# Rebuilding the weight-gradient part of a fused attention and MLP backward kernel in the transposed layout

## The chip, the cores and the metric

The kernel runs on one core of one Trainium2 chip. The metric is the device time of one execution in microseconds (us). A kernel's time is the median of its runs. Each experiment was timed in 3 or 5 rounds beside the kernel before, on the same chip. A ratio is the mean time of one kernel's runs over that of the other's runs of the same rounds, so it isn't quite the ratio of the medians quoted beside it. A profile is one execution; stage lengths come from profiles. Most vary by one or two us from run to run (the pause before dx took 55.9 to 57.2 us in five profiles whose runs don't touch it); the output loop of the changed kernel varies by more, 98.9 to 109.0 us in five profiles with the same loop, nearly all of it in one stall (below).

Engine names as the profile has them: PE is TensorE (matrix products), PEld its weight loads, DVE is VectorE, ACT is ScalarE, POOL is GpSimd, SP is SyncE, which here only issues DMAs. PEclk is the granted TensorE clock as a share of full speed. "DMA share" is the mean busy share of the core's 16 DMA engines (overlapping packets let it go over 1).

## The reference

One attention block and one MLP, joined by a gate, and the gradients of everything. S = 2048 rows, D = 512 columns, 32 heads of 16, F = 1792 hidden columns, all bfloat16.

```python
def _A_ref(x, wqkv, wo):                 # 32 heads of 16, softmax attention
    ...
    return (...).reshape(B, S, D) @ wo
def _B_ref(x, w1, b1, w2, b2):
    y = _layernorm(x)
    h = _gelu(jnp.einsum("bsd,df->bsf", y, w1) + b1)      # tanh form of gelu
    return jnp.einsum("bsf,fd->bsd", h, w2) + b2
xn = _layernorm(x)
s = _A_ref(xn, A_wqkv, A_wo)
g = _silu(_B_ref(xn, B_w1, B_b1, B_w2, B_b2))
out = x + s * g
# wanted: out and jax.vjp for x, wqkv, wo, w1, b1, w2, b2
```

## The kernel before

The program has three parts. A first part (0 to 280 us) makes layer norms, projections and the MLP forward. A hand-scheduled attention, forward and backward in one (280 to 2190 us), follows. The tail (2190 to 2780 us) makes the output, the MLP backward and all weight gradients. The change rewrites the tail.

In the tail, the MLP backward walks over 16 tiles of 128 rows. The hidden activations h lie transposed in DRAM (F on the rows), so each tile is turned on TensorE first, the gelu slope is computed in row layout, and the gradient is turned back for the next product:

```python
def stage_a(t):                              # gelu and its slope for 128 rows
    nc.sync_or_scalar.dma_start(out=h1T[:], in_=k.H1T_s[:, t*128:(t+1)*128]...)   # cut
    for ci, (f0, fn) in enumerate(FCH):      # 14 PE transposes, copied by DVE or ACT
        nc.tensor.transpose(pt[:, b, :], h1T[:, ci*4 + b, :], k.ident_bf[:])
    ... # 2 ACT passes, 3 POOL passes, 5 DVE passes over [128, 1792]
    nc.sync.dma_start(out=k.HG_s[t*128:(t+1)*128, :], in_=hg[:])     # gelu(h), rows
def stage_b(t):
    for ci, (f0, fn) in enumerate(FCH):
        ...                                  # 4 products dm @ w2T into ps
        nc.vector.tensor_tensor(out=dh1[:, f0:f0+fn], in0=ps[:, 0:fn], in1=gp[:, f0:f0+fn], op=ALU.mult)
        for b in range(nb):                  # 14 PE transposes back
            nc.tensor.transpose(pt2[:, b, :], dh1[:, f0+b*128:...], k.ident_bf[:])
        nc.scalar.copy(out=dh1T[:, ci*4:ci*4+nb, :], in_=pt2[:, 0:nb, :])
    nc.scalar.dma_start(out=k.DH1_s[t*128:(t+1)*128, :], in_=dh1[:])
    nc.vector.reduce_sum(out=db1acc[:, t, :], in_=dh1T[:], axis=AX.X)
    ...                                      # 14 products dh1T @ w1T into ps
    ln_bwd_tile(nc, wk, ps[:], y_all[:, t, :], k.rstd2[:, t:t+1], None, dxm_all[:, t, :])
stage_a(0)
for t in range(NT):
    if t + 1 < NT:
        stage_a(t + 1)
    stage_b(t)
```

The layer-norm gradient of a tile runs mostly on POOL, in up to five steps:

```python
def ln_bwd_tile(nc, wk, dy_ps, xhat_bf, rstd_col, extra_add, out_ap, ...):
    ...                                      # row sums s1 (ACT or DVE) and s2 (DVE)
    nc.gpsimd.tensor_scalar(out=ns2[:], in0=s2[:], scalar1=-1.0/D, ...)
    nc.gpsimd.tensor_scalar(out=nms1[:], in0=s1[:], scalar1=-1.0/D, ...)
    nc.gpsimd.tensor_scalar(out=prod[:], in0=xhat_bf, scalar1=ns2[:, 0:1], ...)
    nc.gpsimd.tensor_tensor(out=prod[:], in0=prod[:], in1=dyf[:], op=ALU.add)
    nc.gpsimd.tensor_scalar(out=out_ap, in0=prod[:], scalar1=nms1[:, 0:1], scalar2=rstd_col, ...)
```

The output loop before it keeps the gate tensors of all tiles in memory, turns all 16 tiles of the attention output first, and only then multiplies:

```python
for t in range(NT):
    transpose_to(nc, psT, oT, k.Oall[:, t, :], k.ident_bf, IC, t, t)
for t in range(NT):
    ...                                      # ps = oT(t) @ wo
    nc.vector.tensor_tensor(out=t1[:], in0=ps[:], in1=g_all[:, t, :], op=ALU.mult)
    ...                                      # out = x + t1, stored
    nc.vector.tensor_tensor(out=dm_all[:, t, :], in0=ps[:], in1=B_all[:, t, :], op=ALU.mult)
    transpose_to(nc, psT, dmT, dm_all[:, t, :], k.ident_bf, IC, t, 1)
```

The order of the tail is: output, dwo, weight transposes, MLP backward, dw2, dw1, then dx and dwqkv (with 64 PE transposes of dQ and 128 of dKV).

## Time and profile before

The kernel took 2779.34 us (median of 3 runs, 2777.35 to 2779.35). The profiled execution spans 2779.8 us.

The table of windows gives the busy time of each engine (with instruction counts) in each stretch, then the granted clock, the DMA share and the DMA rate. Kernel before; the first row shown is the attention, then come the stages of the tail: output with dwo and weight transposes, MLP backward, a pause, dw2, dw1, a pause, and the last part.

```profile
core 0: us, PE busy (x) PEld busy (x) DVE busy (x) ACT busy (x) POOL busy (x), PEclk, DMA share, GB/s
...
280.00:2190.00 1910.00, 1773.95 (x15632) 480.41 (x15633) 1548.66 (x2625) 1471.57 (x1538) 267.58 (x699) 0.99 1.15 228
2190.00:2258.00 68.00, 54.09 (x373) 29.78 (x371) 29.37 (x55) 22.55 (x39) 18.65 (x17) 0.90 0.64 212
2258.00:2497.00 239.00, 155.54 (x930) 79.84 (x928) 192.64 (x228) 110.67 (x163) 184.10 (x126) 0.85 0.30 93
2497.00:2521.00 24.00, 1.44 (x12) 1.20 (x12) 1.10 (x2) 1.90 (x1) 2.41 (x3) 0.55 0.50 123
2521.00:2588.00 67.00, 54.22 (x223) 22.26 (x224) 4.84 (x7) 3.52 (x6) 0.00 (x0) 0.91 0.71 176
2588.00:2640.00 52.00, 49.19 (x263) 25.45 (x260) 5.76 (x11) 4.85 (x9) 0.00 (x0) 0.99 0.32 99
2640.00:2663.00 23.00, 4.15 (x41) 3.56 (x40) 1.18 (x3) 4.01 (x8) 0.00 (x0) 0.57 1.01 360
2663.00:2780.00 117.00, 98.78 (x572) 49.41 (x570) 64.03 (x115) 15.66 (x32) 54.88 (x80) 0.98 0.10 33
```

Attention keeps PE busy for 93% of 1910 us, so there is little to win. The tail is 590 us, and its largest piece is the MLP backward: 239 us, in which DVE (192.6 us) and POOL (184.1 us) are busier than PE (155.5 us).

The table of waits says what TensorE stood still for. Kernel before, the tail from 2258 us on:

```profile
engine line waited for: us in total, times, longest us
PE dh_tp L421 <- DVE dh L418: 74.6, 31, 15.7
PE ps_dw L448 <- DMA hgc<-HG_s: 29.2, 9, 16.6
PE kv_tp L509 <- DMA Rkv<-dKVT_s: 18.6, 1, 18.6
```

The first line is the cost of the row layout. TensorE can't turn the gradient back before DVE has multiplied by the slope, and DVE is late. The longest waits of the two lines after it (16.6 and 18.6 us) lie in the two pauses.

### The profile page before, as it was taken

The page shows a single profiled execution, that of the slowest core. Times are in us where ns is not written, and L with a number is a line of the kernel's source. Part 1 is how long each engine was busy: PE and PEld are TensorE (multiplying, and loading weights), DVE is VectorE, ACT ScalarE, POOL GpSimd, SP SyncE. Part 2 cuts the span into 40 slices and gives each one's busy share as a digit, 9 for nine tenths or more (in the row PEclk, how much of TensorE's full clock was granted, in tenths as well). Part 3 has the DMA queues.
Part 4 walks back from the last instruction along what each step waited for, and adds up shares of the span by engine and source line. Part 5 has one row for each costly group of instructions (what it writes and reads, how often), then busy time and mean ns, then how long its engine had stood idle before and what let it go on. Part 6 is the DMA issues. An engine that isn't in the chain of part 4 may idle for free. (4 is left out here: it accounts for less than half of the span.)

```text
span 2779.8 us, 48839 instructions
## 1 busy us (share of the span) xinstructions
PE 2373.2 (85%) x18944; PEld 777.2 (28%) x18944; DVE 2012.5 (72%) x3382; ACT 1736.5 (62%) x1973; POOL 620.4 (22%) x1023
## 2 busy tenths in 40 slices
PE   3786999999999999999999999999999856766967
PEld 2332122222222222222222222222222333322443
DVE  5764688888888888888888888888888638870144
ACT  3343677777777777777777777777777534440020
POOL 0434011111111110111101111111111328870034
PEclk8898799999999999999999999999999978887989
DMA  5434999999999999999999999999999753226331
GB/s 181 108 127 131 197 221 235 226 234 228 231 228 231 236 222 235 225 230 231 230 238 229 226 235 226 234 228 230 227 233 217 208 169 103 96 96 161 106 132 42
DMA packets 1823500, 543.41 MB, mean 195 GB/s; under 512 B 1746593, under 2 KB 1807394, under 8 KB 1823266
## 3 DMA queue, kind: packets, MB, share of 16 engines
q1 hardware_dynamic: 1749874, 486.66, 85.2%
q10 hardware_dynamic: 73392, 53.62, 6.3%
q8 instruction: 148, 2.42, 0.4%
q14 instruction: 86, 0.70, 0.1%
HBM read 65.41 MB, written 55.32 MB: 43 GB/s over the span
## 5 line engine op out<-in xcount | busy, mean ns | idle before, releaser
L699 DVE TENSOR_TENSOR gts<-d,et 128x512 bf16<-128x512 f32 x2048 | 1301.8, 681 | 329.4 <-issue 293.9
L678 ACT ACTIVATE et<-s 128x1024 bf16<-128x1024 f32 x1024 | 997.2, 1023 | 13.1 <-PE d L664 11.7
L686 ACT ACTIVATE e<-t 128x1024 bf16<-128x1024 f32 x512 | 524.3, 1024 | 422.2 <-PE t L636 421.2
L664 PE MATMUL d<-QDT,KVT 32*128 32x512 bf16 x2048 | 597.6, 381 | 115.8 <-DVE gts L699 114.8
L650 PE MATMUL s<-QDT,KVT 32*128 32x512 bf16 x2048 | 401.5, 389 | 14.6 <-DMA QDT<-QDPad 12.6
L730 PE MATMUL X<-et,Lc 128*32 128x512 bf16 x2048 | 401.4, 389 | 14.0 <-DVE xs L751 14.0
L733 PE MATMUL X<-et,NAT 128*32 128x512 bf16 x2048 | 402.0, 389 | 0.0
L745 PE MATMUL X<-gts,NAT 128*17 128x512 bf16 x2048 | 400.5, 387 | 0.0
L814 PE MATMUL Z<-gk,W 128*32 128x512 bf16 x2048 | 394.6, 379 | 0.0
L778 POOL TENSOR_TENSOR W<-NATQd,rL 128x128 bf16<-128x128 bf16 x64 | 25.8, 403 | 1340.7 <-DVE rL L773 1340.7
L745 PEld LDWEIGHTS <-NAT 128*17 128x17 bf16 x2048 | 92.5, 87 | 492.5 <-issue 492.5
L808 PE MATMUL Z<-e,W 128*32 128x512 bf16 x1024 | 200.4, 385 | 3.4 <-DVE acc L821 2.3
L808 PE MATMUL Z<-ek,W 128*32 128x512 bf16 x1024 | 201.3, 389 | 0.0
L636 PE MATMUL t<-KVT,QDT 32*128 32x512 bf16 x1024 | 199.1, 385 | 0.0
L650 PEld LDWEIGHTS <-KVT 32*128 32x128 bf16 x2048 | 96.6, 91 | 356.6 <-issue 356.5
L664 PEld LDWEIGHTS <-KVT 32*128 32x128 bf16 x2048 | 140.1, 91 | 68.5 <-issue 36.9
L730 PEld LDWEIGHTS <-Lc 128*32 128x32 bf16 x2048 | 103.8, 93 | 179.8 <-issue 179.8
L821 DVE TENSOR_TENSOR acc<-Z,acc 64x512 f32<-64x512 f32 x192 | 129.2, 673 | 10.7 <-PE Z L814 10.7
L808 PEld LDWEIGHTS <-W 128*32 128x32 bf16 x2048 | 120.9, 93 | 56.4 <-issue 50.6
L733 PEld LDWEIGHTS <-NAT 128*32 128x32 bf16 x2048 | 100.6, 95 | 50.6
L814 PEld LDWEIGHTS <-W 128*32 128x32 bf16 x2048 | 103.6, 95 | 8.0
L826 POOL CAST ob<-acc 64x512 bf16<-64x512 f32 x64 | 38.8, 607 | 295.3 <-DVE acc L821 295.3
(200 smaller groups left out, 2600.9 us busy)
## 6 DMA issues: line engine op xcount, KB each, us to landing
gk<-gts SPq DMA_TRANSPOSE x512, 4.1
HG_s<-hg SPq DMA_DIRECT2D x16, 448.0 KB, 2.9
DH_s<-dh ACTq DMA_DIRECT2D x16, 448.0 KB, 2.5
NAT<-NAT_s SPq DMA_DIRECT2D x16, 264.0 KB, 3.3
GB_s<-gB ACTq DMA_DIRECT2D x16, 256.0 KB, 2.0
ek<-et SPq DMA_TRANSPOSE x256, 4.2
dKVT_s<-ob SPq DMA_DIRECT2D x16, 256.0 KB, 3.5
dhc<-DH_s ACTq DMA_DIRECT2D x2, 2048.0 KB, 13.2
```

Source lines behind the costliest of these rows:

```text
L636: nc.tensor.matmul(t[:, hj, :], lhsT=op["QDT"][r:r + 32, q0:q0 + 128], rhs=op["KVT"][r:r + 32, kc * 512:(kc + 1) * 512], start=True, stop= ...
L650: nc.tensor.matmul(s[:, hj, :], lhsT=op["KVT"][r:r + 32, kb * 128:(kb + 1) * 128], rhs=op["QDT"][r:r + 32, qc * 512:(qc + 1) * 512], start ...
L664: nc.tensor.matmul(d[:], lhsT=op["KVT"][r:r + 32, kb * 128:(kb + 1) * 128], rhs=op["QDT"][r:r + 32, qc * 512:(qc + 1) * 512], start=True, ...
L678: nc.scalar.activation(out=et[:, :, kb % 4, :, :].rearrange("k b h q -> k h b q"), in_=st_s.pop(g)[:].rearrange("k h (b q) -> k h b q", b= ...
L686: nc.scalar.activation(out=e[:], in_=st_t.pop(g)[:], func=ACT.Exp)
L699: nc.vector.tensor_tensor(out=gts[:, kb % 2, hj, :].rearrange("k (b q) -> k b q", b=4), in0=ds[hj][:].rearrange("k (b q) -> k b q", b=4), ...
L730: nc.tensor.matmul(X[64 + 32 * hj:96 + 32 * hj, :], lhsT=Lc[:], rhs=et[:, :, kb % 4, hj, :], start=(kb == 0), stop=False, skip_group_check ...
L733: nc.tensor.matmul(X[32 * hj:32 * hj + 32, :], lhsT=NATt[:, kb, hj, 1:33], rhs=et[:, :, kb % 4, hj, :], start=(kb == 0), stop=(kb == 15), ...
L745: nc.tensor.matmul(X[64 + 32 * hj:64 + 32 * hj + 17, :], lhsT=NATt[:, kb, hj, 0:17], rhs=gts[:, kb % 2, hj, :], start=False, stop=(kb == 1 ...
L808: nc.tensor.matmul(Z[32 * hj:32 * hj + 32, :], lhsT=blk[j]["W1"][:, qb, hj, :], rhs=ev[:, hj], start=(qb == qb_order[0]), stop=False, tile ...
L814: nc.tensor.matmul(Z[32 * hj:32 * hj + 32, :], lhsT=blk[j]["W2"][:, qb, hj, :], rhs=gv[:, :, :, hj, qb, :], start=False, stop=(qb == qb_or ...
L821: nc.vector.tensor_tensor(out=av, in0=Z[0:64, :], in1=av, op=ALU.add)
```

## The change

The intent: keep the MLP backward in the transposed layout (F on the partitions) from end to end. Then h needs no transpose, the slope is computed on the tensor as it lies, and the two products of the MLP backward chain without turning anything. What must be turned (gelu(h) for dw2, dh for dw1, the weights, dQ, dKV) goes through DMA transposes from DRAM, all on the SP queue. The bias gradient becomes an accumulation in the product's own instruction; the layer norm leaves POOL; the MLP's gradient is added to dx by a product with the identity. To make room in on-chip memory, gate tensors and inputs are loaded per tile, and the output loop becomes one loop per tile, with two of four slope sets free to run beside it. (A slope set holds the gelu slopes of 512 rows, in 7 groups; there are 28 groups in all.) The core of the diff, cut:

```diff
+    def emit_gp(sc):                        # gelu slope, 512 rows, transposed
+        for f0, nf in FG:                   # 7 groups of [128, 2, 512]
+            nc.scalar.dma_start(out=h1[:], in_=k.H1T_s[f0*128:(f0+nf)*128, sc*512:(sc+1)*512]...)
+            ...                             # 3 ACT passes, 7 DVE passes, no POOL
-    for t in range(NT):
-        transpose_to(nc, psT, oT, k.Oall[:, t, :], k.ident_bf, IC, t, t)
     for t in range(NT):
+        transpose_to(nc, psT, oT, k.Oall[:, t, :], k.ident_bf, IC, 0, t)
         ...                                 # ps = oT @ wo
+        (nc.sync if t % 2 == 0 else nc.scalar).dma_start(out=gb[:], in_=k.GB_s[t*128:(t+1)*128, :, :])
         ...                                 # dm, out, dmT as before
+        if t == 3:
+            nc.sync.dma_start_transpose(out=w2T[:], in_=B_w2)
+            nc.sync.dma_start_transpose(out=w1T[:], in_=B_w1)
+    emit_gp(0)
     ...                                     # dwo
+    emit_gp(1)
+    ...                                     # dw2, gelu(h) by nc.sync.dma_start_transpose(out=hgc[:], in_=k.HGT_s[...])
-    stage_a(0)                              # and the row-layout loop over 16 tiles
+    for sc in range(4):                     # 512 rows at a time
+        for fc in range(FC):
+            ...                             # ps = w2T(fc) x dmT
+            nc.vector.scalar_tensor_tensor(out=dh[:, fc, :], in0=ps[:], scalar=1.0, in1=gp[:, fc, :],
+                                           op0=ALU.mult, op1=ALU.mult, accum_out=db1acc[:, sc, fc:fc+1])
+        nc.sync.dma_start(out=k.DH1T_s[:, sc*512:(sc+1)*512]..., in_=dh[:])
+        for tl in range(4):
+            ...                             # ps = dh x w1T, layer-norm gradient
     nc.sync.dma_start(out=out_5.rearrange("(c p) -> p c", p=128), in_=db1[:])
-    ...                                     # PE transposes of wqkv, dQ and dKV
+    nc.sync.dma_start_transpose(out=wT[:], in_=A_wqkv)
+    nc.sync.dma_start_transpose(out=dQT[:], in_=k.dQ_s)
+    nc.scalar.dma_start(out=R[:], in_=k.dKVT_s...)          # then xn_all, dQn
+    nc.sync.dma_start_transpose(out=dKVn[:], in_=k.dKVT_s)
     ...                                     # dx and dwqkv, then dw1 with dhc by DMA transpose
```

The layer norm's new tail end: two tiny DVE operations, one ACT pass with scale and bias, one DVE product (and a POOL addition only in the last part).

## The prediction

> **What bounds the kernel now.** The table of windows splits the 2780 us into three parts: before attention (0 to 280), attention (280 to 2190) and the tail that computes the weight gradients (2190 to 2780, 590 us). The change leaves attention alone except that its gradient store is cut into four small DMAs per pair. In attention the PE is 93% busy, and I expect it unchanged within 10 us. All the gain must come from the tail.
>
> In the tail the PE is busy about 415 of 590 us, and its clock sinks to 0.76 to 0.9 in stages with gaps. The timeline and chain of waits show where the 590 us go: output, dwo and weight transposes 68; the tile loop of the MLP backward 239 (15 us a tile, a ring of POOL, DVE, ACT and PE: POOL ops of 1.5 to 2.6 us, DVE products slowed to 1.2 to 1.7 us beside POOL, a 2.0 us reduction per tile, 448 PE transposes with their copies); 24 of PE idle for a tiny store (15.7 us) and the first reload; dw2 67 with 2 to 5 us DMA waits between columns; dw1 49; 23 of idle for the reload of dKVT; the last part 117, where 76 us are the layer-norm ring on POOL (4.4 us a tile).
>
> **What the change removes.** About 800 of 928 PE transposes (0.06 us each when dense) and their copies; the reduction (now an accumulation in the product); POOL from the gelu slope and nearly all of the layer norm; the dependence between tiles.
>
> **What it adds.** 25 MB of DMA transposes from DRAM on the SP queue. Attention moves 512 KB transposes at 230 GB/s, landing in 4.1 us; the Trainium skill, "DMA: Bandwidth & Descriptors", section "Latency and other measured facts", gives 261 GB/s. From the trace's rate I estimate 4.6 us per MB, so 115 us in all, mostly hidden. That DRAM sources run like SBUF sources is not shown by this trace. Also added: two 3.7 MB stores of the gelu output before attention (0 to 5 us), a dQ round trip, a second sigmoid.
>
> **New tail by stage (estimates).** A dense 512-column matmul costs 0.216 us (dw1 stage).
> 1. Output loop: PE needs 25 us, but the order of instructions puts two of four gelu-slope sets between its DVE products: 14 groups of about 4.4 us (scaled from the 1.09 us uncontended 1792-wide product) plus 26 us: DVE-bound, 85 us, against 68 before.
> 2. dwo and dw2: 288 matmuls, 62 us, plus 3.
> 3. MLP backward: 448 matmuls, 97 us; DVE catches up on the last slope groups: 107.
> 4. Gap: transposed weight, dQ and 4 MB of dKVT must land after the MLP part: 27 of PE idle.
> 5. dx and dwqkv: 400 matmuls, 86 us, with 12 waiting for the 4 MB transposed dKV: 100. dw1: 49. End: 3.
> Sum 434 to 440 instead of 590: about 150 us saved, all on the critical path, since the tail is serial.
>
> **Predicted: 2625 us, range 2560 to 2700.** Faster by over 2%: 0.93; within 2%: 0.05; slower: 0.02.
>
> **What would show it.** Right: MLP backward near 107 us with PE clock above 0.95; no idle over 2 us between dw2 columns; DVE over 85% busy in the output loop while PE is under half; PE idle 20 to 35 us before dx; POOL under 60 us in the tail; attention still 1910 us.
>
> **What would make it wrong.** DRAM transposes at half the assumed rate: then dw2, the gap and dw1 wait on DMA, and up to 90 us are lost (2700). Loads behind 9 us transposes in the SP queue starving the output loop. Better: DVE groups shorter, or the clock at 1.0 throughout (2570). Wrong results from transposes are not expected: all run on one queue.

## The result, and the profile after

The changed kernel took 2690.18 us (median of 4 runs, 2684.70 to 2701.22) against 2778.72 us for the kernel before in the same rounds: ratio 0.969, 95% interval 0.966 to 0.972. Executions over 1.5% slower than the fastest of the same kernel are left out of the means. It is faster by 3.1%, within the predicted range, but 65 us over the predicted point. The profiled run was the fastest of the four (2684.70).

The table of windows of the kernel after (columns as before); the rows shown: attention, output loop, dwo with dw2, MLP backward, a pause, dx with dwqkv, dw1.

```profile
280.00:2190.00 1910.00, 1768.16 (x15620) 480.01 (x15620) 1547.99 (x2624) 1470.54 (x1537) 267.56 (x698) 0.99 1.15 228
2190.00:2292.00 102.00, 55.49 (x201) 18.85 (x202) 76.89 (x126) 53.01 (x62) 22.24 (x16) 0.51 0.76 192
2292.00:2365.00 73.00, 67.31 (x298) 29.22 (x296) 44.00 (x77) 43.13 (x52) 1.53 (x1) 0.95 0.74 162
2365.00:2471.00 106.00, 100.35 (x447) 44.36 (x446) 79.71 (x221) 33.94 (x57) 0.00 (x0) 0.95 0.32 95
2471.00:2527.00 56.00, 1.11 (x6) 0.30 (x4) 3.40 (x10) 2.20 (x4) 0.00 (x0) 0.55 1.06 263
2527.00:2624.00 97.00, 90.14 (x399) 39.96 (x398) 36.75 (x92) 23.69 (x48) 20.51 (x16) 0.95 0.44 119
2624.00:2683.00 59.00, 50.95 (x447) 44.00 (x445) 6.53 (x15) 5.22 (x14) 0.00 (x0) 0.97 0.56 123
```

The balance of the tail, stage against stage, in us:

| | before | predicted | after | after minus predicted |
|---|---|---|---|---|
| output loop | in the next row | 85 | 102 | +17 |
| dwo, dw2 (before: with output and weight transposes) | 68 + 67 | 65 | 73 | +8 |
| MLP backward | 239 | 107 | 106 | -1 |
| PE idle between stages | 24 + 23 | 27 | 56 | +29 |
| dx, dwqkv | 117 | 100 | 97 | -3 |
| dw1 and end | 52 | 52 | 59 | +7 |
| tail | 590 | 436 | 493 | +57 |

The MLP backward does what was hoped: 133 us less, PE busy 95% of it at clock 0.95. Not all of the 133 us is saved work, though: the last operation of a slope group (L319, counted by windows) ran 12 times in the output loop, 9 times in dwo with dw2 and only 7 times in the MLP backward, so 21 of the 28 groups, at some 4.5 us of DVE each, were done before the stage began. Two stages give a part back: the output loop at clock 0.51, and one long pause.

In the views of the loop, dm is the gradient that enters the MLP backward, oT the turned attention output of a tile, and gb a tile's two gate tensors. The waits of TensorE in the output loop, kernel after (columns as in the waits before):

```profile
PE tp_ps L52 <- DVE dm_all L346: 24.6, 15, 12.0
PE ps_so L340 <- DVE oT L54: 16.8, 8, 12.9
PE ps_so L340 <- ACT oT L56: 5.5, 8, 0.7
```

Every turn waits twice, for the product (dm_all) and for a copy (oT). Two waits stand out. The first product waits 12.9 us for a copy that stands on DVE behind slope operations, whose input was still being loaded, and one turn waits 12.0 us for dm while the gate loads stand behind the weight transposes (run 3). The timeline of one turn of that loop, kernel after (start, length, engine, operation; weight loads, slope operations and DMA issues left out), shows why:

```profile
2261.97 0.68 DVE L346 TENSOR_TENSOR dm_all<-ps_so,gb 128x512 bf16<-128x512 f32 x1
...
2262.71 0.61 PE L52 MATMUL tp_ps<-ident_bf,dm_all 128*128 128x128 bf16 x4 [1.13 <-DVE dm_all L346]
2263.25 0.58 PE L353 MATMUL psdb<-dm_all,ones_bf 128*1 128x512 bf16 x1
...
2263.76 0.61 PE L52 MATMUL tp_ps<-ident_bf,Oall 128*128 128x128 bf16 x4
2264.41 0.42 DVE L54 COPY oT<-tp_ps 128x512 bf16<-128x512 bf16 x1 [0.83 <-PE tp_ps L52]
2264.89 1.89 PE L340 MATMUL ps_so<-wo_sb,oT 128*128 128x512 bf16 x4 [0.52 <-DVE oT L54]
2266.82 0.69 DVE L346 TENSOR_TENSOR dm_all<-ps_so,gb 128x512 bf16<-128x512 f32 x1 [0.78 <-PE ps_so L340]
```

This is a ring. PE multiplies, DVE makes dm, PE turns dm, PE turns the next tile of the attention output, DVE or ACT copies it, PE multiplies. From product to product it takes 4.85 us (2261.97 to 2266.82), and the four products take 1.89 us because TensorE is at half clock (1.03 us in turns of run 5 where the clock is up). The first wait, the stall and 16 such turns (some 77 us) are the 102 us of the loop. In the five profiles with this loop the stall took 9.6 to 17.5 us and the rest 89.3 to 91.5 us.

The waits of TensorE from the pause on, kernel after:

```profile
PE ps_dxa L457 <- DMA dQT<-dQ_s: 54.9, 1, 54.9
PE ps_dwq L446 <- DMA dKVn<-dKVT_s: 6.9, 1, 6.9
PE ps_dw L474 <- DMA dhc<-DH1T_s: 4.4, 2, 2.7
```

### The profile page after: what moved, and what is told of

Its sections match the earlier page's. It is cut to its first block, busy times and chain, and to the rows that moved or that the text cites. A ratio compares the mean times of both kernels' runs of the same rounds, so it can differ in the third digit from the quotient of the medians.

```text
span 2682.9 us, 47705 instructions
## 1 busy us (share of the span) xinstructions
PE 2317.8 (86%) x18320; PEld 743.1 (28%) x18320; DVE 1960.5 (73%) x3502; ACT 1733.7 (65%) x1951; POOL 404.5 (15%) x831
## 4 chain that ended last, share of the span: by engine, by line
PE 37%; DVE 37%; issue 14%; DMA 7%; POOL 2%; ACT 1%; SPq 1%; ACTq 0%; DVEq 0%; POOLq 0%
DVE gts L640 29%; PE d L605 6%; PE X L686 6%; PE Z L755 4%; PE Z L749 3%; PE t L577 2%; DVE xs L692 2%; DVE xt L704 2%; PE ps_dhg L405 2%; PE ps_dwq L446 2%; PE XT L702 1%; PE X L671 1%; PE ps_h L212 1%; PE ps_dw L474 1%; PE ps_dw L384 1%
## 5 line engine op out<-in xcount | busy, mean ns | idle before, releaser
L671 PE MATMUL X<-et,Lc 128*32 128x512 bf16 x2048 | 398.0, 385 | 14.3 <-DVE xs L692 14.3
L762 DVE TENSOR_TENSOR acc<-Z,acc 64x512 f32<-64x512 f32 x192 | 129.2, 673 | 13.3 <-PE Z L755 13.3
L577 PEld LDWEIGHTS <-QDT 32*128 32x128 bf16 x1024 | 48.2, 91 | 202.3 <-issue 202.3
```

What stands on the lines that cost most here:

```text
L577: nc.tensor.matmul(t[:, hj, :], lhsT=op["QDT"][r:r + 32, q0:q0 + 128], rhs=op["KVT"][r:r + 32, kc * 512:(kc + 1) * 512], start=True, stop= ...
L671: nc.tensor.matmul(X[64 + 32 * hj:96 + 32 * hj, :], lhsT=Lc[:], rhs=et[:, :, kb % 4, hj, :], start=(kb == 0), stop=False, skip_group_check ...
L762: nc.vector.tensor_tensor(out=av, in0=Z[0:64, :], in1=av, op=ALU.add)
```

## The experiments

Twelve kernels ran, all with results that match the reference. Stage lengths are read from their profiles the same way as above.

### 1. The bias gradient stored in rows (db1rows)

db1 has 1792 values of two bytes. The kernel stores them element by element, while the last tile's y (for the layer norm that must end before anything of the last part may overlay its memory) is being fetched. The edit turns the sums on TensorE and stores 14 rows of 256 bytes.

```diff
-db1 = wk.tile([128, FC], bf16, name="db1")
-nc.vector.tensor_copy(out=db1[:], in_=db1f[:])
-nc.sync.dma_start(out=out_5.rearrange("(c p) -> p c", p=128), in_=db1[:])
+nc.tensor.transpose(db1p[0:FC, 0:128], db1f[:], k.ident_f[:])
+nc.vector.tensor_copy(out=db1[:], in_=db1p[0:FC, 0:128])       # [14, 128]
+nc.sync.dma_start(out=out_5.rearrange("(c p) -> c p", p=128), in_=db1[:])
```

> The changed kernel with one edit: the gradient of b1 is turned by one small PE transpose and stored as 14 rows of 256 bytes, where it was stored as 1792 single elements of 2 bytes (15 us in the DMA rings, 19 to 31 GB/s moved meanwhile). Theory (the element-wise store holds up the rings, so that the last load of a y tile takes 17.5 us, so the last layer-norm tile ends late, so the next part's buffers come free late): the last y load lands in under 4 us, the first dx matmul starts 12 to 17 us earlier, the PE gap before it falls from 55 to 38 to 43 us, the whole by 12 to 17 us (about 2675 us). Rival (the DMA transposes themselves choke the y load): the y load still takes over 12 us and the time stays within 4 us.

Measured: 2678.98 us, ratio 0.9635 (0.9617 to 0.9654), against 0.9687 for the kernel after. The pause went from 56.2 to 45.3 us. Loads of y, kernel after, from the view of that tile (time from issue to landing over the 16 loads):

```profile
DMA to landing us min/median/max: 2.0/2.1/17.5
```

The same of db1rows:

```profile
...
DMA to landing us min/median/max: 2.0/2.0/5.2
```

And the DMA view of the kernel after in 2467 to 2481 us, when that last load was on its way:

```profile
DMA packets 1108, 0.35 MB, mean 25 GB/s; under 512 B 1012, under 2 KB 1108, under 8 KB 1108
```

Little moves in these 14 us, at a DMA share of 0.76. By queue, 996 of the packets (0.25 MB) are on SP's, where the first dh transpose is under way, and 112 (0.10 MB) on ACT's, the y load: this is the traffic that was held up, not the store itself. How the store is cut is seen in the kernel before, where it has SP's queue to itself: the DMA view of 2497 to 2513 us counts 1808 packets with 0.00 MB on that queue, for 1792 values. The Trainium skill, "DMA: Bandwidth & Descriptors", section "Rules for kernel authors", says that a non-contiguous last dimension lowers to one descriptor per element; this trace agrees. In the kernel after, the store of 3.5 KB took 21.3 us to land and held up a 128 KB load that takes 2.1 us otherwise. This is 11 us of the pause, shown; how so small a store holds the others up is not.

### 2. The first dh transposes later (dhclate)

Next to that store, two transposes of dh (for dw1) were issued some 150 us before their use. Were they what delayed the y load?

```diff
-nc.sync.dma_start_transpose(out=dKVn[:], in_=k.dKVT_s)
+last_tr = nc.sync.dma_start_transpose(out=dKVn[:], in_=k.dKVT_s)
 ...
+with tc.issue_after(last_tr.ins):
     nc.sync.dma_start_transpose(out=dhc[:], in_=k.DH1T_s[f0:f0 + 256, :])
```

> The changed kernel with one edit: the first two transposed loads of dh for the dw1 part are queued behind the transposes of the qkv weight, dQ and dKV, not ahead of them. Theory (the element-wise store is the culprit of the first 15 us, and the rest of the gap is bandwidth for the operands of the next part, which can't be loaded before the last layer-norm tile is done): the last y load still takes over 12 us, the gap falls by 0 to 5 us only. Rival (the order in the SP queue costs the gap): the y load lands in under 4 us, the gap falls by 15 to 20 us.

Measured: 2685.68 us, ratio 0.9661 (0.9644 to 0.9678). The last y load still took 14.3 us, the pause was 52.0 us. So the transposes count for some 4 us, and the element-wise store for the larger part.

### 3. The weight transposes later (wlate)

In the output loop, the loads of the gate tensors stand behind the transposes of w2 and w1 on the SP queue (11.7 and 8.1 us of issue in the kernel after).

```diff
-if t == 3:
-    nc.sync.dma_start_transpose(out=w2T[:], in_=B_w2)
-    nc.sync.dma_start_transpose(out=w1T[:], in_=B_w1)
+if t == 12:
+    with tc.issue_after(o0_dma.ins):         # behind tile 12's output store
+        ...                                  # the same two
```

> The changed kernel with one edit: the transposed loads of w2 and w1 (20 us of the SP queue) are queued behind the output store of tile 12, not after tile 3. Theory (the output loop of 101 us holds 12 us of waiting for loads stuck behind these two; beyond that it is bound by VectorE): no PE wait over 5 us at tile 5, the loop takes 88 to 94 us, the whole falls by 6 to 12 us. Rival (the loop is bound by VectorE alone, and the wait only moves its work): loop within 4 us of 101.

Measured: 2675.67 us, ratio 0.9625 (0.9606 to 0.9644). The loop went from 101.8 to 92.8 us (98.9 to 109.0 in the five profiles with the old order). The 12 us stall at tile 5 is gone: no wait for dm is longer than 2.0 us. The rest of the loop still runs at half clock (0.52) with its ring.

### 4. A slope set moved out of the loop (gplate)

The prediction called the loop DVE-bound, since slope operations run beside it. This edit keeps the second set behind the loop's last product.

```diff
-emit_gp(1)
+with tc.issue_after(last_dve.ins):          # last_dve: t1 of the last tile
+    emit_gp(1)
```

> The changed kernel with one edit: the second gelu-slope set may not start before the output loop's last product on VectorE. Theory (in the loop VectorE is in order and works on slopes that are not needed for another 100 us, while PE waits): the loop falls from 101 to 75 to 82 us; the MLP backward grows from 110 to 115 to 130, as VectorE has 233 us of work from the end of attention to the gap against PE's 184; net 8 to 20 us faster. Rival (the total of VectorE's work bounds this stretch, wherever it is placed): the loop shrinks, the MLP part grows by the same, the whole within 4 us.

Measured: 2702.04 us, ratio 0.9717 (0.9698 to 0.9735), no faster than the kernel after (0.9687; the intervals overlap, so it isn't shown to be slower). This is the run that takes the prediction's model of the loop down. Its loop, table of windows (columns as before):

```profile
2190.00:2298.00 108.00, 53.35 (x197) 18.50 (x200) 54.25 (x89) 37.74 (x47) 19.93 (x16) 0.53 0.76 169
```

DVE work fell from 76.9 to 54.3 us, and the loop did not shrink. Its 108.1 us hold a stall of 17.8 us; without the stall it is 90.3 us, against 89.8 us in the kernel after. The slopes came back in the MLP backward, which rose from 106.3 to 118.4 us.

### 5. The loop staggered over three tiles (pipe)

Same instructions, only TensorE's order is fixed: turn the attention output of tile t, multiply tile t-1, turn dm of tile t-2. (oT gets three buffers of its own.)

```diff
-for t in range(NT):
-    ...                                     # turn O(t), multiply, turn dm(t)
+for i in range(NT + 2):
+    if i < NT: stage_o(i)                   # transposes of O(i), copy to oT
+    if 1 <= i <= NT: stage_s(i - 1)         # products, dm, t1, output
+    if i >= 2: stage_m(i - 2)               # transposes of dm, db2 product
+    # each TensorE instruction: tc.keep_in_program_order(...)
```

> The changed kernel with the output loop staggered over three tiles: in each turn TensorE transposes the attention output of tile t, multiplies tile t-1, and transposes the product of tile t-2; the same instructions, only TensorE's order is fixed. Theory 'one in-order ring': the output loop (101.8 us, VectorE busy 76.5 us of it) is long because every tile runs TensorE, VectorE, TensorE, copy, TensorE in sequence, so the loop falls to about 78 to 85 us (then VectorE's own work holds it) and the whole to about 2668 to 2675 us. Rival 'VectorE's order': the slope operations that stand ahead of the products on VectorE, and their loads, set the pace; the loop stays above 95 us and the whole above 2683 us.

Measured: 2672.14 us, ratio 0.960 (0.9585 to 0.9614). Table of windows, the loop of this run:

```profile
2190.00:2273.00 83.00, 39.82 (x205) 17.89 (x206) 48.46 (x81) 32.98 (x42) 19.77 (x16) 0.63 0.89 213
```

The loop fell from 101.8 to 82.2 us, as the ring theory has it. A part of this is the rival's: the first product starts 6.8 us after the attention's last, against 13.3 us in the kernel after, since the first copies no longer stand behind slope operations on DVE. And a part came back: only 5 slope groups ended in this loop, 10 were left for the MLP backward (7 in the kernel after), and that stage took 114.6 us. But my reason for stopping at 80 us, DVE's own work, is wrong: DVE is busy for 48.5 of 83 us. The largest wait of TensorE in this loop:

```profile
PE tp_ps L373 <- DVE dm_all L362: 32.9, 5, 13.2
```

There are five waits for dm now, up to 13.2 us long, not one per tile. What DVE itself waits for in the same loop is the gate tensors' loads (same view, DVE):

```profile
DVE dm_all L362 <- DMA gb<-GB_s: 19.1, 4, 10.0
```

In the timeline, these loads stand behind the w2 and w1 transposes on SP.

### 6. Staggered, and the slope set out of the loop (pipegp)

The edits of 5 and 4 together.

> The staggered loop, and the second set of gelu slopes kept behind the loop's last product on VectorE. Theory 'one in-order ring': without those slopes the staggered loop has about 45 us of VectorE work and falls to 55 to 65 us; but the slopes come back in the MLP stage (118 us in the earlier run with only this move, against 106), so the whole is 2660 to 2672 us, within 10 us of the staggered loop alone. Rival 'TensorE at the low clock holds the loop': some 4 us of TensorE per tile at half clock keep the loop at 65 us or more whatever VectorE has to do, and the whole is above 2675 us.

Measured: 2669.91 us, ratio 0.9592 (0.9575 to 0.961). The loop took 77.1 us, the MLP backward 115.0 us. Neither theory has both numbers: the loop isn't at 55 to 65 us, and the whole isn't above 2675 us. The edit moved little, since in run 5 too only 5 slope groups ended in the loop; so this run says little about DVE. The granted clock rose to 0.73 (0.63 in run 5) and the loop fell by 5 us only, so half clock is not the whole limit of this version. I took the loads to be: DVE waits 18.1 us for gate tensors, and the DMA share is 0.94 at 227 GB/s. Run 10 tests that.

### 7. Two operands of the last part fetched early (early)

db1rows, plus the transposed attention weights (1.5 MB) and dQ (2 MB) fetched during the MLP backward into memory of their own.

```diff
+pR = c1.enter_context(tc.tile_pool(name="p3_early", bufs=1, side="right"))
+wT = pR.tile([128, 12, D], bf16, name="wqkvT"); dQT = pR.tile([128, IC, S], bf16, name="dQT")
 for sc in range(4):
     ...
+    if sc == 1:                             # behind the dh store
+        nc.sync.dma_start_transpose(out=wT[:], in_=A_wqkv)
+        nc.sync.dma_start_transpose(out=dQT[:], in_=k.dQ_s)
```

> The changed kernel with the 14-row bias store and with the transposed attention weights and the transposed query gradient (1.5 and 2 MB) fetched during the MLP stage into memory of their own, so that they aren't part of the burst at the stage change. Theory 'bytes of the burst': the gap before the first input-gradient product falls from 45 us (bias store alone) to 18 to 26 us, and the whole from 2679 to 2652 to 2662 us. Rival 'a serial chain after the last layer norm': the gap stays at 38 us or more and the whole within 8 us of 2679 us.

Measured: 2661.40 us, ratio 0.9553 (0.9533 to 0.9572), against 0.9635 for db1rows. The first dx product follows the MLP backward at once, and the waiting moved inside the last part, which grew from 95.6 to 116.4 us. The pause is thus about 21 us (0.5 + 116.4 - 95.6) instead of 45.3: the theory of bytes holds in this sum, though the gap itself, 0.5 us, is not where the theory had it. The MLP backward grew by 7 us to 113.5; why, I didn't settle.

What these bytes are is seen in the DMA view of the kernel after, 2489 to 2527 us, the second part of its pause:

```profile
DMA packets 21558, 12.65 MB, mean 333 GB/s; under 512 B 16310, under 2 KB 20534, under 8 KB 21558
...
Rkv<-dKVT_s ACTq DMA_DIRECT2D x1, 4096.0 KB, 13.5
xn_all<-XN_s ACTq DMA_DIRECT2D x1, 2048.0 KB, 20.3
dQn<-dQ_s ACTq DMA_DIRECT2D x1, 2048.0 KB, 26.9
```

For 38 us the DMA engines are full (share 1.10) and TensorE has nothing to do. The 1.5 MB transpose of the weights, first in the SP queue, took 25 us to issue because it shared the engines with 8 MB of plain loads, and dQT waited behind it.

### 8. Only the new layer norm, in the old kernel (newln)

The layer-norm gradient leaves POOL and the MLP's gradient is added by an identity product; everything else is the kernel before. The function is the new one shown under the change; the call sites:

```diff
-ln_bwd_tile(..., k.rstd1[:, t:t+1], dout_all[:, t, :], dx[:], add_src=dxm_all[:, t, :])
+nc.tensor.matmul(ps[:], lhsT=k.ident_bf[:], rhs=dxm_all[:, t, :], start=True, stop=False)
+ln_bwd_tile(..., k.rstd1[:, t:t+1], dx[:], extra_add=dout_all[:, t, :])
```

> The kernel before with only one part of the change: the layer-norm gradient moved off GpSimd (the new five-step form), and the MLP gradient added through an identity product. If the layer norm on GpSimd (81 of its 184 us in the MLP stage, 55 us in the last) is what held those stages, the MLP stage falls from 239 to about 200 us, the last from 117 to about 103 us, and the whole to 2715 to 2730 us. If it is VectorE (192 of 239 us busy, and the new form gives it one operation more per tile) and the transposes of the row layout, the MLP stage stays above 220 us, and the whole is 2745 us or more: then the layout, not the layer norm, is where the saving came from.

Measured: 2773.98 us against 2784.46, ratio 0.9967 (0.9952 to 0.9981). Its MLP backward, and its last part, from the table of windows:

```profile
2251.00:2504.00 253.00, 161.77 (x981) 89.47 (x998) 196.33 (x276) 125.29 (x184) 104.14 (x48) 0.81 0.32 94
...
2674.00:2776.00 102.00, 97.36 (x560) 49.47 (x568) 52.52 (x114) 36.93 (x79) 20.29 (x16) 0.99 0.11 37
```

POOL lost 79 us in the MLP backward, and that stage became longer: 253 us against 243 for the same stretch (2251 to 2494) before. The last part did become 14 us shorter. So the layer norm was not what cost the 239 us. That the row layout was, with DVE at 196 us and TensorE waiting for it, follows by elimination only: its transposes, its reduction and its slope work were not taken out one at a time.

### 9. The old layer norm in the changed kernel (oldln)

```diff
-nc.vector.tensor_scalar(out=ab[:, 0:1], ...)     # and the rest of the new form
+nc.gpsimd.tensor_scalar(out=ns2[:], ...)         # the old form, on POOL
```

> The changed kernel with only the layer-norm gradient put back on GpSimd in its old form. Theory 'the new layout, not the layer norm, made the MLP stage short': GpSimd has about 5 us a tile, 81 us in the MLP stage of 106 us, where it is otherwise idle, so the stage grows by no more than 8 us; the last part grows by 5 to 15 us, because its tiles come every 3.4 us in fours; the whole is 2695 to 2710 us. Rival 'the layer norm is a large part of the gain': MLP stage and last part together grow by 30 us or more, the whole above 2718 us.

Measured: 2702.58 us, ratio 0.9704 (0.9684 to 0.9724), against 0.9687 for the kernel after: 5 us by the ratios, whose intervals overlap, and 12 by the medians. The MLP backward took 110.2 us (106.3), as expected; the last part did not grow (95.8 us), though I had expected 5 to 15 us; dw1 took 62 us instead of 56, which I can't explain. In the new layout the place of the layer norm is nearly free.

### 10. A version meant to beat both (best)

The staggered loop, the weight transposes behind tile 12, the rows of db1, and dw1 moved: right after the MLP backward, with y and two blocks of dh fetched before, so that the operands of the last part load while TensorE has work. dwqkv starts at tile 9.

```diff
+y_all = pR.tile(...); dhp2 = ...(bufs=2, side="right")     # in the MLP stage
+if sc == 3: load_dhc(0); load_dhc(1)
+for ci in range(7):                          # dw1 before dx
+    ...                                      # 4 x 16 products, 4 stores
+    if ci + 2 < 7: load_dhc(ci + 2)
+    ...                                      # wT after block 0, dQT after block 1, dKVn in 4 pieces from block 4
-if t % 4 == 3: dw_qkv(t // 4)
+if t >= 9 and t % 2 == 1: dw_qkv((t - 9) // 2)
```

> The version meant to beat both: the changed kernel with the staggered output loop, the transposes of the MLP weights moved behind the loads of tile 12, the 14-row bias store, and the weight gradient dw1 done right after the MLP stage (its operand y and the first two blocks of dh fetched during that stage into memory of their own), so that the 14 MB for the last part load while TensorE has work; the products for dwqkv come from tile 9 on. If the output loop is held by its in-order ring and by loads behind the weight transposes, it falls to 60 to 72 us (from 101.8). If the gap is bytes waiting with no work left, it goes to the end of dw1 and shrinks to 10 to 20 us (from 56), as some 66 us of transfers stand against 50 us of products. The whole: 2600 to 2630 us. If instead one serial queue of transposes (some 46 us of issue for dw1's and the two operands of dx) holds dw1, that stage is over 75 us instead of 56, and the whole is 2630 us or more.

Measured: 2652.89 us, ratio 0.9522 (0.9498 to 0.9547). The output loop:

```profile
2190.00:2254.00 64.00, 34.36 (x210) 15.74 (x207) 39.98 (x64) 25.54 (x35) 18.81 (x16) 0.80 0.86 208
```

It took 63 us, at clock 0.80, so staggering the ring and moving the weight transposes together took off 39 of its 102 us. Some slope work left the loop with them (DVE is busy 40 us in it, against 77), but run 4 showed that this alone gains nothing. But dw1 took 97 us instead of 56, as the second alternative had it, and the whole missed 2600 to 2630. The waits of the tail:

```profile
PE ps_dw L490 <- DMA dhc<-DH1T_s: 34.6, 5, 15.9
PE tp_ps L373 <- DVE dm_all L362: 22.6, 6, 14.8
PE ps_dhg L446 <- DVE dh1T L448: 17.0, 7, 6.3
```

The third line is a shorter loop's price: DVE's slope work (some 4.5 us a group, 28 groups) is the same, and what isn't done beside the loop is done in the MLP backward, now 123 us.

### 11. The same with staggered loads (best2)

The 8 MB of plain loads no longer start together, but one by one behind dw1's copies; the third slope set may start before dw2, and y is loaded from SP's queue instead of ACT's.

```diff
-nc.scalar.dma_start(out=R[:], ...); nc.scalar.dma_start(out=xn_all[:], ...); nc.scalar.dma_start(out=dQn[:], ...)
+if ci in act_loads:                          # R in halves at 0 and 1, xn at 2, dQn at 5
+    with tc.issue_after(act_copy.ins):
+        act_loads[ci]()
```

> The version before with two edits: the 8 MB of loads for the last part are no longer issued at once at the end of the MLP stage but one by one behind copies of the dw1 blocks (4 MB in two halves, then 2 MB, then 2 MB), and the third set of gelu slopes may start before dw2. In the version before, the second dh block took 17.7 us to issue and 25 us to land beside those 8 MB, and TensorE waited 34.6 us for dh blocks in the 97 us of dw1. Theory 'the order of the transfers, not their number': the transfers stay the same in sum, the dw1 stage falls to 62 to 72 us and the wait for dh blocks to 5 to 15 us; the last part stays at 86 to 92 us. Rival 'bytes, or the single queue of transposes': the same bytes take the same time, the dw1 stage stays at 88 us or more. The slopes: the MLP stage, 123 us, falls to 108 to 118 us if VectorE finds work in the dw2 stage, else it stays. The whole: 2612 to 2632 us by the first theory, above 2642 us by the rival.

Measured: 2651.77 us, ratio 0.9528 (0.9503 to 0.9552): no change. dw1 took 93 us, the MLP backward 123 us. The theory of the order of transfers falls. I read the dw1 stage as held by SP as an in-order queue: its turns held four stores of dw1 (3.6 to 5.0 us), a dh transpose (4.4 to 9.4 us) and at times a big transpose, and DMA was busy for only 0.89 of the stage (211 GB/s).

### 12. dw1's stores off the transposes' queue (best3)

Beside the lines below, dh blocks are fetched up to four ahead and the big transposes are issued in another order (wqkv before dw1's first block, dKV's pieces from block 2 on).

```diff
-dw1 = wk.tile([128, 256], bf16, name="dw1")          # 2 buffers
-nc.sync.dma_start(out=out_4[...], in_=dw1[:])
+dw1 = dwp.tile([128, 256], bf16, name="dw1")         # 6 buffers
+nc.scalar.dma_start(out=out_4[...], in_=dw1[:])
+spare = {2: dKVn[:, :, 768:1024], 3: dKVn[:, :, 512:768], 6: dKVn[:, :, 768:1024]}
```

> The last version with three edits in dw1: its 28 stores of 64 KB leave on ScalarE's queue instead of the queue that carries the transposes; there are six buffers for them instead of two; and blocks 2, 3 and 6 of dh are transposed into the still empty memory of the dKV operand, so that four blocks can be under way instead of two. In the version before, the queue was taken in turn by four stores (3.6 to 5.0 us), a dh transpose (4.4 to 9.4 us) and the big transposes (6.3 and 8.1 us), about 95 us in the 93 us of the dw1 stage. Theory 'one in-order queue': 25 us of stores leave it, some 60 to 65 us of transposes stay, the dw1 stage falls to 58 to 70 us and the whole to 2618 to 2632 us. Rival 'bytes': the same 16 MB with the transposes at a lower rate hold the stage, it stays above 80 us and the whole above 2638 us.

Measured: 2634.03 us (2626.66 to 2635.98, 5 runs), ratio 0.9462 (0.9445 to 0.9479), beside 2781.52 for the kernel before. It is the fastest version, 5.4% under the kernel before. The dw1 stage, table of windows:

```profile
2468.00:2543.00 75.00, 54.19 (x449) 46.11 (x450) 6.61 (x15) 4.94 (x13) 0.00 (x0) 0.84 1.19 273
```

From the end of the MLP backward to the first dx product it is 77 us (93 before this edit): between the two theories. The edits together were worth 16 us; how much of it is the queue and how much the buffers, the fetching ahead and the new order was not separated. What is left, from the waits of TensorE in this stretch (2455 to 2560 us):

```profile
PE ps_dw L498 <- ACT dw L504: 11.1, 1, 11.1
PE ps_dw L498 <- DMA dKVn<-DH1T_s: 9.6, 1, 9.6
```

The DMA share is now 1.19, so bytes are one limit. The longest wait, though, is for ScalarE's copy of a finished block, on the engine that now issues the stores and the plain loads too; no run tested which of the two holds the stage. The stores could leave the queue, the transposes couldn't: the Trainium skill, "DMA: Bandwidth & Descriptors", section "Silent corruption: two transposing streams in flight at once", warns of wrong data when two queues transpose at the same time. No run here shows it; all runs kept the transposes on one queue and were correct.

## Why the prediction was right or wrong

**Right: direction and range.** All the gain is in the tail; attention stayed at its 1910 us with PE busy 1768 us (1774 before).

**Right: the MLP backward, 107 predicted, 106 measured**, PE clock 0.95, POOL 44 us in the tail (predicted under 60). The mechanism named, the loss of transposes and of the ring from tile to tile, is supported by runs 8 and 9, which rule out the layer norm: the new one alone saves 10 us in the old layout, and the old one costs 5 to 12 us in the new (not clear of noise). The parts of the new layout were not tested one by one. There is some luck in the 106 us: 21 of 28 slope groups were done before the stage, 12 of them in an output loop that was slower than predicted. When fewer were done before (runs 4, 5, 6 and 10, with 8, 10, 10 and 12 groups left), the stage took 114.6 to 123 us.

**Wrong: "Output loop ... DVE-bound, 85 us".** It took 102 us with DVE busy 75% of it (predicted over 85%) and PE 54% (predicted under half). Taking 23 us of DVE work away didn't shorten it (run 4); staggering it took 20 us (run 5); moving the weight transposes took 9 us, the stall (run 3); both together brought it to 63 us (run 10). The prediction had named "loads behind 9 us transposes in the SP queue starving the output loop" as a risk, and that came true as the stall of 12.0 us; it had not followed the order of TensorE's instructions, which makes a ring of 4.85 us a tile, some 77 of the 102 us. The slope work on DVE did hold the loop at one place, its first product (12.9 us).

**Wrong by its size: the pause before dx, 27 predicted, 56 measured.** The step was right (operands must land when no work is left), two terms were mis-sized. The store of 1792 single elements was seen in the profile before (15.7 us for the same 3.5 KB) and left in the new sum as if it cost nothing; it delays the last layer norm by 11 us (run 1). And the rate: 4.6 us per MB was taken from attention for each transpose, as if it had the DMA engines to itself. The weights' 1.5 MB took 25 us beside the plain loads. It is the sum that counts: the prediction's line names 7.5 MB (weights, dQ, dKV), but xn and the rows of dQ, 4 MB more, were loaded beside them and the transpose of dKV had begun; 12.65 MB at 333 GB/s are 38 us.

**Right where it was alone: the rate of DRAM transposes.** A 1 MB transpose of dh takes 4.4 us to issue and lands after 6.4 us (medians of seven in the kernel after; the first, inside the pause, took 15.6 and 19.2), near the 4.6 us estimated from attention's on-chip sources. So the worry that DRAM sources are half as fast fell. "No idle over 2 us between dw2 columns" was slightly off: waits for gelu(h) came to 2.9, 1.8 and 0.6 us.

**Small terms:** dwo with dw2 8 us more (a clock of 0.95, and those waits), dw1 with the end 7 us more (4.4 us of waits for dh).

So of the 154 us expected, 97 were measured in the profiles; of the 57 missing, 29 lie in the pause and 17 in the output loop, both shown by runs that change them; 15 are in dwo, dw2 and dw1, read from the waits alone; 4 came back elsewhere.

## What to carry to other kernels

When DMA transposes replace TensorE transposes, add up the bytes of each stage change and divide by the rate of all DMA engines together; a transpose's own rate says little where 8 MB of loads start beside it, and a queue that carries long transposes should carry nothing that a loop waits for. A loop over tiles in which one engine appears three times per tile should be staggered, in that engine's order of instructions, before another engine's load is blamed. After taking a bottleneck away, look where its work went: the slope work that left the output loop came back in the MLP stage in runs 4, 5, 6 and 10.

## What the Trainium skill lacked or had wrong

- "DMA: Bandwidth & Descriptors", section "Latency and other measured facts", gives 261 GB/s for a DMA transpose with a non-contiguous middle dimension (a condition that the prediction left out); it has no figure for transposes beside plain loads. Here a 1.5 MB transpose took 25 us of issue beside 8 MB of loads (and 6.3 us in run 11, with the loads spread out), and transposes and loads together moved 333 GB/s.
- "Advanced Engine Details and Errata", section "X-Bar Transpose (TRN2)", says that transpose DMAs are as fast as regular DMAs. Attention, full of 512 KB transposes, moved 228 GB/s at a DMA share of 1.15, while the pause's mix of loads and transposes moved 333 GB/s at 1.10: here they were slower. In the pause, SP's queue (transposes) took 49.2% of the engines for 4.13 MB, ACT's (plain loads) 61.3% for 8.52 MB.
- "DMA: Bandwidth & Descriptors", section "Rules for kernel authors", has the one descriptor per element, but not what it does to others: a 3.5 KB store held a 128 KB load for 14.3 us instead of 2.1 us, with no transpose beside it (run 2).
- "TensorE: Matmul & The Clock Gate", section "HAM oscillation — how this bites in real kernels", has loops that lose the clock at every wait for DMA, and the page tells of short idles between groups of products too; it has no figure for a ring through other engines like this one. Here it had clock 0.50 from 2210 to 2270 us with PE busy about 70% of the time in turns without stalls, and 0.80 for the same instructions staggered and fed (run 10). Whether its short transposes or its pauses keep the clock down wasn't separated.
- No page gives the time for which a transpose of 1 to 4 MB from DRAM takes its in-order issuing queue from everything behind it (4.3 to 25 us of issue here); run 3 shows a stall of 12 us for it, and run 12 16 us together with its other edits.
